# A GEGLU and spectral-mixing kernel: one product of the next chunk moved into the tail of the down projection, part of the down projection moved ahead of the last gate/up product, and silu of the last chunk by one ACT function

## The chip, the cores and the metric

The kernel runs on one core of a Trainium2 chip. The metric is the device time of one execution in microseconds (us). The kernel before the change took 1782.99 us (median of 3 runs, 1782.35 to 1784.18). The engines are called as in the profile: PE multiplies matrices (PEld is its weight load), DVE is the vector engine, ACT the activation engine, POOL the second, slower vector engine, and SP the queue that issues nearly all DMAs.

## The reference

The input x has 8192 tokens of 448 values. With xn the layer norm of x, the result is

```
s = irfft(shrink(mlp(rfft(xn over the tokens))))        # block-diagonal complex MLP, 4 blocks of 112
g = silu((gelu(xn @ w_gate) * (xn @ w_up)) @ w_down)    # 448 -> 1792 -> 448
out = x + s * g
```

Everything is float32. The kernel reaches float32 accuracy with float16 matmuls: each operand is split into a high and a low half, and a product takes three matmuls (high by high, high by low, low by high).

## The kernel before, in words

**Work.** The 8192 tokens are laid out as 128 x 64, and a *chunk* is 4 of the 64 columns, 512 tokens; there are 16 chunks, numbered i = 0 to 15. The FFN runs in two parts over the hidden units: part p = 0 has hidden blocks 0 to 7 (of 128), part p = 1 blocks 8 to 13. Part 0 of all chunks comes first and leaves partial sums in DRAM (`prt`); part 1 reads them back (tile `pt`), adds its own, and gives silu. From some point of part 0 on, both the gate/up projections and the down projection use a fast scheme with 7 instead of 8 block products.

**Gate/up** (`unit`, line 1108). Two hidden blocks make a unit; part 1 has 3 units in a chunk. A unit's 7 products are the generators a1, a5, a6, a4, a2, a3, a7. They accumulate in two PSUM banks, X (ring `bx`) and Y, Z (ring `by`), and between them ACT or DVE work on the banks: `seed` copies X after a1, `sum5` adds after a6 (DVE, `by<-bx,u`), `c22` adds after a7 (DVE, `v<-bx,u`), and a4 adds into X only when that addition has read it. After a4 comes gelu, the multiplication by up, and `sums` (line 1208), which makes the left operands of the down projection. A product on the X side that reads tile `xta` is 12 matmuls of 256 columns; one that reads `xtb` (a2, a3, a4) is 10.

**Down** (`down2`, line 1355, and `prod2`, line 1322). The 7 products are prod2(1) to prod2(7); each has 6 matmuls of 224 columns for each unit of the chunk. They accumulate in banks x and y (ring `bd`) and z (ring `by`). Banks are read in the middle: `add2` (DVE, `pt<-bd`) adds the bank to the partial sum of one quadrant of the chunk, and after that the next product adds on into the same bank. The part called `tail` is not run at the end of the chunk but within the next one, after a1 and a5 of its first unit: it finishes prod2(6) in bank x and prod2(5) in bank y, then waits for `add2` of x, and goes on with prod2(7) in x, prod2(3) in y and prod2(4) in x. Each quadrant that is complete goes to `ended2` (line 1454): `add2`, then tanh by ACT on half the value, and (1 + tanh) times the half by DVE, which is silu. The last chunk has no next one, so its tail follows at once, and its last product is cut in two halves (`last_half`, line 1437).

**Side work.** The spectral branch runs beside the FFN in three phases that fill gaps: phase 1 (layer norm, first DFT stage, operands of the FFN, one chunk each `DT` us from `T1` on), phase 2 (second DFT stage, MLP, shrinkage, third stage; 64 tasks spread evenly up to `END2`), and phase 3 (last DFT stage, multiplication by silu, adding x, the store; spread up to `END3`). In phase 3, chunks whose FFN is done by then take silu from DRAM (`gsp`) in tiles of two columns; later chunks multiply at once (`gate`, line 1422), called direct here.

**What sets the order.** Nothing is scheduled by the compiler. The kernel writes every engine's instructions in the order of a plan: `Pace` (line 50) runs the generators as tasks against a model of the engines (line 172) and of DMA (line 136), and the order in which they reach an instruction is the order on the engine. Each engine then runs its list in order and waits on semaphores. The choice of DVE or POOL for an operation written as `B.` (line 209) is the plan's too. So any change of a constant of the plan may reorder the side work everywhere after it.

Of the kernel before, what the change touches and what calls it, by code (L numbers as in the profile page):

```python
# [13 lines left out]
AF = mybir.ActivationFunctionType  # L14
ALU = mybir.AluOpType
# [6 lines left out]
NG = 16  # L22
# [7 lines left out]
PF = ((0, 8), (8, 6))  # L30
# [19 lines left out]
class Pace:  # L50
# [85 lines left out]
    def issue(self, e, op, out, ins, run):  # L136
        outs, ins, start = self.start(e, out, ins)
        if e == "SP" or op == "dma_start":
            size = (outs or ins)[0].nbytes()
            self.dma = max(self.dma, start) + size / 320e3  # L140
            if op == "dma_start_transpose":
                self.free[e] = start + 1.15 + size / 380e3
                end = max(self.free[e] + 2.6, self.dma + 1.5)
            else:
                self.free[e] = start + 0.5
                end = max(start + 2.2 + size / 240e3, self.dma + 1.5) + (2.5 if outs and start > 100.0 else 0.0)
        else:
            end = start + self.cost(e, op, start, out, ins)
            self.free[e] = end
            if self.shares(e, op, out, ins):  # L150
                self.port[e] = self.port[e][-11:] + [(start, end)]
        for i in ins:
            self.note(i, False, end, e)
        for o in outs:
            self.note(o, True, end, e)
        self.last = max(self.last, end)
        return run()
# [234 lines left out]
def afno_geglu_kernel(ctx, tc, x, gu, wd, mlp, b1, b2, c_m, c_mt, c_small, out):  # L392
# [4 lines left out]
    B = Either(pace, V, G, 0.0)  # L397
# [32 lines left out]
    def pe():  # L430
        return pace.free.get("PE", 0.0) - 0.3
# [16 lines left out]
    wt = [cp.tile([128, 2, 16, 128], F16, name=f"wt{f}") for f in range(PF[0][1])]  # L448
    dw = [cp.tile([128, PF[0][1], D], F16, name=f"dw{i}") for i in range(2)]
    ms = cp.tile([128, 32], F32, name="ms")  # L450
    cB = [fb[:, 0:1], fb[:, 1:2]]
    cF = ms[:, 24:25]

# [209 lines left out]
            if c + 1 < NG + PL:  # L663
                yield ev("phase", c)

    T1, DT = 84.0, 37.0


    def gu_loads(fs, again):
# [411 lines left out]
    state = {"direct": NG}  # L1081
# [26 lines left out]
    def unit(p, i, f0, h, xa, seven):  # L1108
# [87 lines left out]
        def c21():  # L1196
            gl = yield from (GL if p == 0 else GL2).get()
            gelu(p, f0, gl, m["X"])
            BX.put(m["X"])
            yield  # L1200
            yield from glu(p, seven, f0, gl, m["v2"], 1, h, lambda: V2.put(m["v2"]))
            if seven:
                yield from sums(gl)
                return
            GL.put(gl)
            done("h", p, i, f0, 1)
# [148 lines left out]
    def down2(p, i, h, last):  # L1355

        n = PF[p][1] // 2
        yield from last()
        x = yield from BD.get()
        yield from prod2(1, p, i, h, x, 0, n - 1, first=True)  # L1360
        z = yield from BY.get()
        yield from prod2(2, p, i, h, z, 0, n - 1, first=True)
        T.matmul(z[:, 2 * DH:], h[:, 0, 0, 0:128], dw[0][:, 0, 0:512 - 2 * DH], start=False, stop=False,
                 skip_group_check=True)
        y = yield from BD.get()
        yield from prod2(5, p, i, h, y, 0, n - 2, first=True)
        yield from prod2(1, p, i, h, x, n - 1, n)
        e = pace.spawn(add2(p, i, QS[0], x), pace.last)
        yield from prod2(2, p, i, h, z, n - 1, n, last=True)
        pace.spawn(ended2(p, i, QS[0], z, BY, e), pace.last)  # L1370
        yield from prod2(5, p, i, h, y, n - 2, n - 1)
        yield e
        yield from prod2(6, p, i, h, x, 0, n - 1)

        def tail():
            yield from prod2(6, p, i, h, x, n - 1, n)
            e = pace.spawn(add2(p, i, QS[2], x), pace.last)
            yield from prod2(5, p, i, h, y, n - 1, n)
            e5 = pace.spawn(add2(p, i, QS[1], y), pace.last)
            yield e  # L1380
            yield from prod2(7, p, i, h, x, 0, n)
            pace.spawn(ended2(p, i, QS[1], x, None), pace.last)
            yield e5
            yield from prod2(3, p, i, h, y, 0, n, last=True)
            pace.spawn(ended2(p, i, QS[2], y, BD), pace.last)
            yield ev("u3", p, i)
            if p == 0 or i < NG - 1:
                yield from prod2(4, p, i, h, x, 0, n, last=True)
                pace.spawn(ended2(p, i, QS[3], x, BD), pace.last)
                return  # L1390
            tf = yield from TH.get()
            for t in range(2):
                yield from prod2(4, p, i, h, x, 0, n, last=True, halves=(t,))
                pace.spawn(last_half(i, QS[3], x, tf, t), pace.last)

        state["tail"] = tail
# [40 lines left out]
    def last_half(i, qq, b, tf, a):  # L1437

        v = slice(a, a + 1)
        q, s4 = EV["ptb", i, qq][:, v], blk(state["last"], *qq)[:, v]  # L1440
        x4 = EV["lgt", i, qq[0]][-1][:, v, DH * qq[1]:DH * qq[1] + DH]
        th = tf.rearrange("p (a d) -> p a d", a=2)[:, v]
        V.scalar_tensor_tensor(q, part(b, 128, 2, DH)[:, v], cB[1], q, op0=ALU.mult, op1=ALU.add)
        yield
        S.activation(th, q, AF.Tanh)
        B.tensor_mul(s4, q, s4)
        yield
        V.scalar_tensor_tensor(th, th, 1.0, s4, op0=ALU.add, op1=ALU.mult)
        yield
        B.tensor_add(th, th, x4)  # L1450
        yield
        Q.dma_start(blk(ov[:, CH * i:CH * i + CH, :], *qq)[:, v], th)

    def ended2(p, i, qq, b, R, earlier=None):

        if earlier:
            yield earlier
        if p == 1 and state["direct"] <= i < NG - 1:
            pace.spawn(gate_bank(i, qq))
        yield from add2(p, i, qq, b)  # L1460
        if R:
            R.put(b)
        else:
            done("u3", p, i)
        if p == 0:
            t, v = EV["ptb", 0, i, qq]
            Q.dma_start(blk(chunk_of(prt, i), *qq), v)
            TH.put(t)
            return
        q = EV["ptb", i, qq]  # L1470
        tf = yield from TH.get()
        th = tf.rearrange("p (a d) -> p a d", a=2)
        S.activation(th, q, AF.Tanh)
        if i < NG - 1:
            yield
            V.scalar_tensor_tensor(th, th, 1.0, q, op0=ALU.add, op1=ALU.mult)
            PT.put(q)
            yield
            if i >= state["direct"]:
                yield from gate(i, qq, th)  # L1480
                Q.dma_start(blk(ov[:, CH * i:CH * i + CH, :], *qq), th)
                TH.put(tf)
                return
            Q.dma_start(blk(chunk_of(gsp, i), *qq), th)
            TH.put(tf)
            EV["gn", i] = EV.get(("gn", i), 0) + 1
            if EV["gn", i] == 4:
                done("gsp", i)
            return
        for a in range(qq[0], CH, 2):  # L1490
            yield ev("s4", a)
        yield ev("lg", i, qq[0])
        yield ev("hs", 1, i, PF[1][1] - 2, 0)
        s4, x4 = blk(state["last"], *qq), EV["lgt", i, qq[0]][-1][:, :, DH * qq[1]:DH * qq[1] + DH]
        B.tensor_mul(s4, q, s4)
        yield
        V.scalar_tensor_tensor(th, th, 1.0, s4, op0=ALU.add, op1=ALU.mult)
        yield
        V.tensor_add(th, th, x4)
        PT.put(q)  # L1500
        yield
        Q.dma_start(blk(ov[:, CH * i:CH * i + CH, :], *qq), th)
        TH.put(tf)
# [78 lines left out]
    def chunk(p, i):  # L1582
# [26 lines left out]
        for u, (_, a5, a6, a4, a2, a3, a7) in enumerate(units):  # L1609
            yield from a5()  # L1610
            yield pe()
            if u == 0 and "tail" in state:
                yield from state.pop("tail")()
                if (p, i) == (1, 0):
                    factors_in(1)
                    open_mq()
                    pace.spawn(xt_load(nxt[1], "a", nxt[0]))
                    pace.spawn(pt_loads(i))
            yield from a6()
            yield pe()  # L1620
            if u == 0:
                yield ev("xt", "b", p, i)
            else:
                yield from prev()
                if (p, i) == (0, NG - 1):
                    pace.spawn(far_pair(u - 1))
                yield pe()
            yield from a2()
            yield pe()
            for s in (a3, units[u + 1][0], a7) if u + 1 < len(units) else (a7, a3) if seven else (a3, a7):  # L1630
                yield from s()
                yield pe()
            prev = a4
# [300 lines left out]

            pace.spawn(store())

    END1, END2, END3 = T1 + NG * DT + 12.0, 1460.0, 1765.0

    def phase2():
        yield ev("phase1")  # L1940
# [445 lines left out]
```

## Time and profile before

| | before |
|---|---|
| median of 3 runs | 1782.99 us |
| the profiled execution's own time | 1784.63 us |
| its span, first to last instruction | 1782.8 us |
| granted clock of PE | 0.997 |
| PE, share of the span busy | 99% |
| DVE | 78% |
| ACT | 58% |
| POOL | 32% |
| DMA, mean rate | 160 GB/s |

The span leaves out what lies around the first and last instruction; the execution's own time is 1.8 us longer. All lines of helper calls have one line number (204), so the groups are told apart by the names of their tiles. A row of a timeline gives start, duration, engine, operation, tiles, number merged, and in brackets the idle time of the engine before it and what ended that. PE's matmul ends are modelled; the idle time of PEld shows more directly how long PE's stream stood still.

### The profile page before, as it was taken

Reading aid. Unit: us, or ns where it says so; the run is one execution under the profiler, and the core shown is the slowest. Engines: PE = TensorE matmul, PEld = TensorE weight load, DVE = VectorE, ACT = ScalarE, POOL = GpSimd, SP = SyncE. Lnnn points to the kernel's source line nnn. Section 1 sums busy time; section 2 is a strip of 40 time slices with the busy share of each in tenths; the row PEclk is TensorE's granted clock in tenths of the full one; section 3 lists DMA queues with packets and bytes.
Section 4 is the critical chain, followed back from the end, with each engine's and each line's share of the span. In section 5 each row is a group of like instructions: output and inputs, shape, how many; then the busy total and the mean of one; then the engine's idle time right before and its main releaser. Section 6 shows DMA issues by size and latency. Waiting matters only on the chain.

```text
span 1782.8 us, 40305 instructions
## 1 busy us (share of the span) xinstructions
PE 1759.6 (99%) x16183; PEld 1470.3 (82%) x16183; DVE 1392.9 (78%) x2471; ACT 1031.5 (58%) x2019; POOL 570.4 (32%) x689
## 2 busy tenths in 40 slices
PE   8999999999999999999999999999999999999998
PEld 4447677777787799999999999999999998988887
DVE  7879777777776676767778788888888887888877
ACT  6646555546555545666767666777666663333333
POOL 3153444555542542222212123333132321121211
PEclk9999999999999999999999999999999999999999
DMA  6465776677766653323147554434354438999871
GB/s 216 133 179 166 185 217 181 189 225 202 214 188 178 182 141 82 79 64 90 53 100 208 156 121 111 109 90 103 92 121 110 99 96 262 285 294 306 260 263 53
DMA packets 354892, 285.37 MB, mean 160 GB/s; under 512 B 235184, under 2 KB 324784, under 8 KB 354704
## 3 DMA queue, kind: packets, MB, share of 16 engines
q1 hardware_dynamic: 354416, 282.24, 55.8%
q8 instruction: 126, 2.06, 0.5%
q14 instruction: 62, 0.51, 0.1%
q10 hardware_dynamic: 288, 0.56, 0.1%
HBM read 128.36 MB, written 105.23 MB: 131 GB/s over the span
## 4 chain that ended last, share of the span: by engine, by line
PE 93%; DVE 4%; DMA 1%; ACT 1%; issue 1%; POOL 0%; SPq 0%; ACTq 0%; DVEq 0%; POOLq 0%
PE bx L204 31%; PE by L204 23%; PE bd L204 22%; PE bf L204 16%; DVE wt L204 1%; DMA prt<-th 1%; DVE g L204 1%; DVE pt L204 1%; ACT wt L204 0%; SPq L204 0%; DMA out<-th 0%; DVE v L204 0%; DVE th L204 0%; DMA x<-in_x 0%; ACT th L204 0%
## 5 line engine op out<-in xcount | busy, mean ns | idle before, releaser
L204 PEld LDWEIGHTS <-wt 128*128 128x128 f16 x9350 | 906.7, 98 | 172.3 <-issue 16.7
L204 PE MATMUL bx<-xta,wt 128*128 128x256 f16 (+1 forms) x3843 | 476.2, 275 | 3.0 <-ACT by L204 1.2
L204 PEld LDWEIGHTS <-h 128*128 128x128 f16 x2710 | 260.1, 98 | 83.5 <-issue 2.4
L204 PE MATMUL bd<-dw,h 128*128 128x448 f16 (+1 forms) x1596 | 254.1, 310 | 1.1 <-DVE pt L204 0.8
L204 PE MATMUL by<-xtb,wt 128*128 128x256 f16 x2080 | 252.6, 273 | 2.0 <-DVE by L204 2.0
L204 PE MATMUL by<-xta,wt 128*128 128x256 f16 (+1 forms) x1347 | 177.2, 279 | 0.8 <-DVE xta L204 0.8
L204 POOL TENSOR_TENSOR wt<-wt 128x256 f32<-128x256 f32 x80 | 63.1, 789 | 297.8 <-DVE wt L204 279.8
L204 PE MATMUL bx<-xtb,wt 128*128 128x256 f16 x1040 | 130.5, 272 | 1.8 <-DVE v L204 1.8
L204 DVE TENSOR_TENSOR by<-bx,u 128x512 f32<-128x512 f32 x104 | 72.5, 697 | 61.9 <-PE bx L204 53.0
L204 ACT COPY u<-by 128x512 f32<-128x512 f32 x104 | 60.8, 584 | 86.3 <-PE by L204 86.0
L204 POOL TENSOR_TENSOR zs<-t,zs 112x256 f16<-112x256 f32 (+1 forms) x38 | 31.7, 835 | 243.5 <-ACT zs L204 243.5
L204 PE MATMUL bd<-dw,wt 128*128 128x224 f16 (+1 forms) x816 | 99.4, 264 | 2.7 <-DVE pt L204 2.5
L204 ACT ACTIVATE u<-by,fc 128x512 f32<-128x512 f32 (+1 forms) x118 | 73.6, 635 | 49.2 <-PE by L204 49.0
L204 ACT CAST h<-wt 128x512 f16<-128x512 f32 (+1 forms) x128 | 68.6, 536 | 48.8 <-DVE wt L204 40.1
L204 DVE TENSOR_TENSOR v<-bx,u 128x512 f32<-128x512 f32 x104 | 71.4, 686 | 21.5 <-PE bx L204 20.4
L204 ACT COPY by<-bx 128x512 f32<-128x512 f32 x104 | 59.7, 574 | 44.9 <-PE bx L204 44.4
L204 PE MATMUL bf<-w2t,wn 112*128 112x112 f16 x1512 | 84.9, 213 | 0.0
L204 DVE SCALAR_TENSOR_TENSOR pt<-bd,fb,pt 128x448 f32<-128x448 f32 (+1 forms) x97 | 65.0, 675 | 23.7 <-PE bd L204 22.9
L204 PEld LDWEIGHTS <-wn 112*128 112x128 f16 x1512 | 80.6, 98 | 1.0
L204 ACT ACTIVATE th<-pt 128x448 f32<-128x448 f32 (+1 forms) x65 | 37.1, 571 | 73.9 <-DVE pt L204 67.7
L204 ACT ACTIVATE th<-bd,fb 128x448 f32<-128x448 f32 x62 | 39.1, 633 | 64.8 <-PE bd L204 62.8
L204 ACT ACTIVATE gl<-bx,fc 128x512 f32<-128x512 f32 (+1 forms) x70 | 40.6, 600 | 56.8 <-PE bx L204 49.8
(263 smaller groups left out, 3332.2 us busy)
## 6 DMA issues: line engine op xcount, KB each, us to landing
xts<-sx SPq DMA_DIRECT2D x32, 480.0 KB, 3.9
x<-in_x SPq DMA_DIRECT2D x17, 896.0 KB, 6.3
t<-ysb SPq DMA_DIRECT2D x64, 224.0 KB, 3.1
prt<-th SPq DMA_DIRECT2D x64, 224.0 KB, 2.5
pt<-prt SPq DMA_DIRECT2D x64, 224.0 KB, 3.8
u<-t SPq DMA_DIRECT2D x32, 448.0 KB, 5.9
x<-in_x SPq DMA_DIRECT2D x32, 448.0 KB, 6.4
y<-t SPq DMA_DIRECT2D x30, 448.0 KB, 3.6
```

Of the source, the lines that this page charges most:

```text
L204: return self.pace.issue(self.name, kind, out, ins, lambda: fn(out, *args, **kw))
```

## The change

1. In `down2`, the first unit's share of prod2(1), 6 matmuls into bank x, is put ahead of `last()`, which is a4 of the chunk's last unit. It came after it.
2. In `tail`, the next chunk's a6 (of its first unit) is put between prod2(5) and the wait for `add2` of x. It came after the whole tail. The last chunk's tail has no such product.
3. In the last chunk silu is one ACT function on the half value with scale 2, then a multiplication by the spectral factor and an addition of x, both by DVE. Before, it was tanh, a multiplication of the half value by the spectral factor (DVE or POOL), (1 + tanh) times that, and the addition (DVE or POOL). An ACT instruction on one column, put after the last gelu, brings in the function's table.
4. Constants of the plan: loads are modelled as landing 0.5 us later, `DT` goes from 37.0 to 36.5, `END2` from 1460 to 1480. `END3` stays at 1765.

```diff
-                end = max(start + 2.2 + size / 240e3, self.dma + 1.5) + (2.5 if outs and start > 100.0 else 0.0)
+                end = max(start + 2.2 + size / 240e3, self.dma + 1.5) + (3.0 if outs and start > 100.0 else 0.0)
...
-    T1, DT = 84.0, 37.0
+    T1, DT = 84.0, 36.5
...
+            if (p, i, f0) == (1, NG - 1, PF[1][1] - 2):
+                S.activation(fb[:, 4:5], mhalf1, AF.Silu)
...
+        x = yield from BD.get()
+        yield from prod2(1, p, i, h, x, 0, 1, first=True)
         yield from last()
-        x = yield from BD.get()
-        yield from prod2(1, p, i, h, x, 0, n - 1, first=True)
+        yield from prod2(1, p, i, h, x, 1, n - 1)
...
-        def tail():
+        between = []
+
+        def tail(mid=None):
+            between.extend([mid] if mid else [])
             yield from prod2(6, p, i, h, x, n - 1, n)
             e = pace.spawn(add2(p, i, QS[2], x), pace.last)
             yield from prod2(5, p, i, h, y, n - 1, n)
             e5 = pace.spawn(add2(p, i, QS[1], y), pace.last)
+            if between:
+                yield from between[0]()
+                yield pe()
             yield e
...
-        S.activation(th, q, AF.Tanh)
-        B.tensor_mul(s4, q, s4)
-        yield
-        V.scalar_tensor_tensor(th, th, 1.0, s4, op0=ALU.add, op1=ALU.mult)
-        yield
-        B.tensor_add(th, th, x4)
+        S.activation(th, q, AF.Silu, scale=2.0)
+        yield
+        V.tensor_tensor(th, th, s4, op=ALU.mult)
+        yield
+        V.tensor_tensor(th, th, x4, op=ALU.add)
...
-        S.activation(th, q, AF.Tanh)
+        S.activation(th, q, AF.Silu if i == NG - 1 else AF.Tanh, scale=2.0 if i == NG - 1 else 1.0)
...
-        B.tensor_mul(s4, q, s4)
-        yield
-        V.scalar_tensor_tensor(th, th, 1.0, s4, op0=ALU.add, op1=ALU.mult)
-        yield
-        V.tensor_add(th, th, x4)
+        yield
+        V.tensor_tensor(th, th, s4, op=ALU.mult)
+        yield
+        V.tensor_tensor(th, th, x4, op=ALU.add)
...
-            if u == 0 and "tail" in state:
-                yield from state.pop("tail")()
+            ahead = u == 0 and "tail" in state
+            if ahead:
+                yield from state.pop("tail")(a6)
...
-            yield from a6()
-            yield pe()
+            if not ahead:
+                yield from a6()
+                yield pe()
...
-    END1, END2, END3 = T1 + NG * DT + 12.0, 1460.0, 1765.0
+    END1, END2, END3 = T1 + NG * DT + 12.0, 1480.0, 1765.0
```

More of the change, by code (lines that the diff above doesn't have):

```diff
@@ L450, in afno_geglu_kernel @@
     ms = cp.tile([128, 32], F32, name="ms")
+    mhalf1 = mhalf[:, 0:1]
     cB = [fb[:, 0:1], fb[:, 1:2]]
```

## The prediction, on record before the result

> **What bounds the kernel now.** I read the page first: who is busy.
>
> ```profile
> PE 1759.6 (99%) x16183; PEld 1470.3 (82%) x16183; DVE 1392.9 (78%) x2471; ACT 1031.5 (58%) x2019; POOL 570.4 (32%) x689
> ```
>
> PE is the bound: 1759.6 of 1782.8 us. The change adds and removes no matmul, so it can win only what PE stands still, and what follows PE's last matmul. Next, the busy time of long stretches: two of phase 2, then phase 3, then the end (us, then busy time and count of PE, PEld, DVE, ACT, POOL, clock, DMA share, GB/s).
>
> ```profile
> 712.00:1112.00 400.00, 399.59 (x4348) 369.34 (x4346) 310.01 (x563) 270.10 (x562) 97.50 (x99) 1.00 0.42 109
> 1112.00:1472.00 360.00, 358.78 (x3899) 331.62 (x3898) 302.42 (x529) 245.62 (x500) 105.94 (x106) 1.00 0.43 104
> 1472.00:1732.00 260.00, 256.19 (x2353) 227.97 (x2351) 210.46 (x334) 94.65 (x166) 52.24 (x59) 1.00 0.90 278
> 1732.00:1783.00 51.00, 43.20 (x404) 38.74 (x402) 36.77 (x63) 19.09 (x34) 6.52 (x8) 0.97 0.26 82
> ```
>
> The clock is full. In phase 3 DMA is busy at 0.90 where it was at 0.43, and DVE at 210.46/260 = 0.81. PE's idle time is small, so the third view is what PEld waited for, from 630 to 1472 us and then from 1472 to 1735 us (us in total, times, longest).
>
> ```profile
> PEld L204 <- issue: 3.9, 11, 0.8
> ...
> PEld L204 <- issue: 5.3, 9, 1.8
> ```
>
> So PE stood still for 9.2 us in 20 places over the stretch in which the scheme of 7 products runs. I followed each in the timeline. They are of three kinds: 8 stand in the tail of the down projection, 3 before the a4 of a chunk's last unit, and 9 elsewhere. The change goes at the first two kinds.
>
> **The tail (part 2).** The pace of matmuls comes from two pieces of the chain that ended last: 24 of 256 columns in 2.62 us, 0.109 us each; 18 of 224 columns in 1.73 us, 0.096 us each.
>
> ```profile
> 1733.22 1.73 PE bd L204 x18
> ...
> 1741.87 2.62 PE bx L204 x24
> ```
>
> A typical tail, PE and then DVE:
>
> ```profile
> 1592.35 1.31 PE L204 MATMUL bd<-wt,h 128*128 128x224 f16 x12
> 1593.87 0.35 PE L204 MATMUL bd<-dw,wt 128*128 128x224 f16 x2 [0.20 <-DVE pt L204]
> ```
>
> ```profile
> 1593.13 1.28 DVE L204 SCALAR_TENSOR_TENSOR pt<-bd,fb,pt 128x448 f32<-128x448 f32 x2 [0.43 <-PE bd L204]
> ```
>
> The 12 matmuls are prod2(6) in x and prod2(5) in y. After the first 6 (0.57 us) DVE may read x; it starts at 1593.13 and its first addition takes half of 1.28 us. But prod2(5) covers only 0.57 us of it, and 12 x 0.096 = 1.15 us after 1592.35 PE is out of work, at 1593.50. It goes on at 1593.87: 0.37 us lost. The 8 such places, the first and the last (PEld's rows, idle time in brackets):
>
> ```profile
> 652.57 0.48 PEld L204 LDWEIGHTS <-h 128*128 128x128 f16 x5 [0.31 <-issue]
> ...
> 1730.19 0.86 PEld L204 LDWEIGHTS <-wt 128*128 128x128 f16 x9 [0.36 <-issue]
> ```
>
> Two are of 0.31 (part 0), six of 0.36 to 0.38: 2.8 us. Between them lie tails without a wait, in which the plan happened to put a matmul of the side work there. The change puts a6 there: 12 x 0.109 = 1.31 us, over three times what is missing, so all 8 go, even with DVE almost 1 us late. What is late next? a6 itself needs only `seed`, done long before; its `sum5` puts one more DVE addition (about 0.7 us) into the tail, behind both `add2`, and a3 needs it five products later. Bank y's `add2` gains the same cover. a2 now follows prod2(4) at once and needs Z and `xtb`, whose load was issued a whole down projection earlier. prod2(7), 3, 4 and their stores come 1.31 us later. I cost these at nothing: nothing in the next 4 us of PE waits for them. **-2.8 us.**
>
> **The head (part 1).** PE, DVE and PEld before an a4, the last with the first such place too:
>
> ```profile
> 1624.91 1.25 PE L204 MATMUL by<-xtb,wt 128*128 128x256 f16 x10
> 1626.59 0.60 PE L204 MATMUL bx<-xtb,wt 128*128 128x256 f16 x4 [0.43 <-DVE v L204]
> ```
>
> ```profile
> 1625.86 0.68 DVE L204 TENSOR_TENSOR v<-bx,u 128x512 f32<-128x512 f32 x1
> ```
>
> ```profile
> 639.32 0.75 PEld L204 LDWEIGHTS <-wt 128*128 128x128 f16 x7 [0.36 <-issue]
> ...
> 1626.60 0.97 PEld L204 LDWEIGHTS <-wt 128*128 128x128 f16 x9 [0.60 <-issue]
> ```
>
> a4 has to wait until DVE has read X (`v<-bx,u`, end 1626.54), and a3 alone is 1.09 us of cover. Six matmuls of prod2(1) add 0.57 us. The three waits (0.36, 0.36 and 0.60) make 1.32 us, of which 0.03 stays: **-1.3 us**. The operands of prod2(1) come from the first unit and bank x has been free since the tail, so nothing is newly waited for; a4's own results come 0.57 us minus the saved wait later, and the next tail, which needs them, has a1 and a5 (2.6 us) ahead of it.
>
> **The last chunk (parts 1 to 3).** Here no next chunk covers the tail. PEld waited 0.36 us for the same a4:
>
> ```profile
> 1761.54 0.53 PEld L204 LDWEIGHTS <-wt 128*128 128x128 f16 x5 [0.36 <-issue]
> ```
>
> With 0.57 us in front a4 starts 0.21 us later, and the chain of waits at the end runs through what follows a4 (gelu, `sums`, tail): **+0.2 us**. On ACT the rows after that a4, and the only table load of the trace:
>
> ```profile
> 1763.07 0.69 ACT L204 ACTIVATE wt<-bx,fc 128x512 f32<-128x512 f32 x1
> 1764.86 0.41 ACT L204 CAST h<-wt 128x256 f16<-128x256 f32 x1 [1.10 <-DVE wt L204]
> 1765.77 0.62 ACT L204 CAST h<-wt 128x512 f16<-128x512 f32 x1 [0.51 <-DVE wt L204]
> ```
>
> ```profile
> 1.65 1.28 ACT L204 ACT_TABLE_LOAD   x1 [1.65 <-PEq L2377]
> 2.95 0.20 ACT L204 ACTIVATE fb<-mhalf 128x1 f32<-128x1 f32 x1
> ```
>
> The new instruction follows the gelu. Load and one column take 1.28 + 0.20 = 1.48 us and the gap is 1.10, so the first cast is 0.38 us late; the second has 0.51 us to spare, so 0.13 us is left over: nothing. The Trainium skill (ScalarE: Activation LUTs, section "What ACT_TABLE_LOAD costs") gives a drain of about 1.38 us on top of the 1283 ns. The trace shows the 1283 ns, and behind it the next instruction at once; no run here shows a load in the middle of work. By the page the second cast would be 1.25 us late, and the sum 1.25 us higher.
>
> The end, on DVE and POOL (the last matmul starts at about 1776.6):
>
> ```profile
> 1776.64 0.38 DVE L204 TENSOR_TENSOR s<-pt,s 128x224 f32<-128x224 f32 x1
> 1776.94 0.44 DVE L204 SCALAR_TENSOR_TENSOR pt<-bd,fb,pt 128x224 f32<-128x224 f32 x1
> 1777.30 1.38 DVE L204 SCALAR_TENSOR_TENSOR th<-th,s 128x448 f32<-128x448 f32 x2
> 1778.61 0.91 DVE L204 TENSOR_TENSOR th<-th,x 128x448 f32<-128x448 f32 x2
> 1779.44 0.38 DVE L204 SCALAR_TENSOR_TENSOR th<-th,s 128x224 f32<-128x224 f32 x1
> 1779.86 0.39 DVE L204 TENSOR_TENSOR th<-th,x 128x224 f32<-128x224 f32 x1
> ```
>
> ```profile
> 1777.46 0.98 POOL L204 TENSOR_TENSOR s<-pt,s 128x224 f32<-128x224 f32 x1 [1.22 <-DVE pt L204]
> ```
>
> From `pt` on DVE needs 3.31 us (1776.94 to 1780.25), and POOL's 0.98 us lies within it. After the change the last half needs pt 0.44, silu (as tanh of this size, about 0.4; silu isn't in the trace, and I take it between that and twice that), a multiplication 0.38 and an addition 0.39: 1.6 us and some 0.1 for hand-offs, so up to 1.6 us less. If DVE still has to do the two additions before (0.91 in the rows) it is 2.6 us, 0.7 us less. I take **-1.0 us**, with -1.6 and, by a doubled silu in all three dependent places, +0.2 as ends.
>
> **The plan (part 4).** Phase 2 ends 20 us later and starts about 8 us earlier (16 x 0.5), so its 64 tasks thin out by about 4%; the five of the 9 others that lie before 1472 us sum to about 1.8 us (3.9 less 1.7 in tails and 0.36 before an a4), and I take **-0.3**. Phase 3 has the same work in 240 instead of 260 us: DMA 0.90 x 260/240 = 0.97, DVE 0.81 to about 0.84. The four remaining waits there sum to 3.2 us (5.3 less 1.1 and 0.96), the largest of them this one, where ACT waited for a store, DVE for ACT, and PE for DVE:
>
> ```profile
> 1693.88 0.58 ACT L204 ACTIVATE th<-pt 128x448 f32<-128x448 f32 x1 [3.50 <-DMA out<-th]
> ```
>
> ```profile
> 1695.77 0.31 PEld L204 LDWEIGHTS <-wt 128*128 128x128 f16 x3 [1.80 <-issue]
> ```
>
> I let them grow by a quarter, **+0.8**; bounds are -1.6 (half of them vanish in a new order) and +9 (below). The 0.5 us on loads only puts their users later in the order: 0, since no wait of PE on DMA stands in the trace. Phase 1's order before 215 us is drawn anew as well; I take 0, within 2 us either way.
>
> **The sum.** -2.8 - 1.3 + 0.2 - 1.0 - 0.3 + 0.8 = -4.4 us. From the profiled execution, 1784.63 to 1780.2. The median lies 1.64 us below that execution: 1782.99 - 4.4 = 1778.6 us.
>
> **Rivals.**
> *DVE is the real bound of the tails.* If DVE, at 0.81 in phase 3, gets to `add2` over 1 us late, the wait stays in front of prod2(7), or moves to a3. For it: rows show DVE starting an addition late elsewhere. Against: at 1593.13 DVE was idle for 0.43 us before it. It takes back the 2.8 us and leaves 1781.4.
> *Phase 3 is too tight: slower.* Stores land later at a DMA share of 0.97, all three buffers of `th` are in flight, ACT stops as at 1693.88, and each such stop costs PE 1.80 us. From one stop in each of the five direct chunks (10 to 14) on it decides: 5 x 1.80 = 9.0 against -5.2 for the rest, 1786.8. For it: DMA at 0.90 already. Against: one stop in 20 stores before, and moving the quadrants 1.31 us apart from the first gives its store more time.
> *The table load is longer, or is on the path.* Every microsecond beyond the gap is paid at the end. With a second load's worth, 1.28 us, it is 1779.9. The page's drain comes to about the same.
> *The stage boundary flips.* Ten chunks take silu from DRAM:
>
> ```profile
> gsp<-th SPq DMA_DIRECT2D x40, 224.0 KB, 2.5
> ```
>
> 40 stores, four a chunk. If phase 3 begins after chunk 10's start, an eleventh follows: 1.8 MB more, at 278 GB/s 6.6 us of DMA, PE's work unchanged. I count it to the slower rival's causes.
>
> **How the numbers follow.** Forecast (both covers hold, 1774 to 1781) 0.62; DVE bound 0.16, at 1781.4; phase 3 too tight 0.13, at 1786.8; table load 0.09, at 1779.9. A measurement here can tell about 0.2%, 3.6 us. Faster by more (below 1779.4): 0.60 of the forecast, 0.03 of the table load and 0.03 of the DVE case, 0.66; slower by more (above 1786.6) half or more of the third, 0.10; the same 0.24. The range leaves out about 2 in 10: from 1773.5 (the end at -1.6, waits halved and 2 us in phase 1) to 1783.0 (DVE bound and 1.6 us of phase 3).
>
> **What would show it.** Right: no PEld wait between prod2(5) and prod2(7) but in the last tail; `bx<-xta` as 12 matmuls there; no wait before the last unit's a4; one more table load; under 3 us from the last `pt` to the last addition; 40 stores to `gsp`. Wrong: waits on `pt` or `by` after 1490 us that sum to over 8 us, ACT waiting for `out<-th` several times, or new waits between 84 and 630 us.

## The result, and the profile after

| | before | after |
|---|---|---|
| median | 1782.88 us (6 runs, 1782.03 to 1784.18) | 1776.34 us (6 runs, 1775.42 to 1776.92) |
| ratio | | 0.9963, 95% interval 0.9950 to 0.9976 |
| the profiled execution's own time | 1784.63 us | 1775.42 us |
| its span | 1782.8 us | 1773.6 us |

The change makes the kernel 6.5 us faster by the medians; 4.4 were forecast, and 1776.34 lies within the range. Mind the two profiled executions: that of before lies 1.75 us above its median, that of after 0.92 below, so the traces differ by 9.2 us and about 2.7 of that is the spread of executions.

The page after, its first line:

```profile
PE 1758.0 (99%) x16183; PEld 1469.4 (83%) x16183; DVE 1401.5 (79%) x2482; ACT 1032.0 (58%) x2021; POOL 532.5 (30%) x673
```

PE has as many matmuls and all but the same busy time. DVE has 11 instructions more and POOL 16 fewer. The gain is PE's idle time and the end. The stretches after, with phase 3 now from 1494 us on:

```profile
712.00:1112.00 400.00, 399.86 (x4333) 369.45 (x4331) 312.79 (x558) 270.79 (x558) 86.63 (x100) 1.00 0.43 108
1112.00:1494.00 382.00, 381.71 (x4135) 352.90 (x4134) 323.75 (x561) 258.42 (x524) 99.63 (x107) 1.00 0.42 103
1494.00:1732.00 238.00, 237.50 (x2199) 212.54 (x2197) 196.01 (x318) 85.02 (x150) 42.83 (x49) 1.00 0.96 293
1732.00:1774.00 42.00, 35.59 (x326) 31.20 (x324) 32.04 (x54) 17.85 (x32) 6.90 (x9) 0.97 0.37 126
```

In phase 3 the share of DMA went from 0.90 to 0.96 (0.97 was worked out), and yet PE's idle time there fell from 3.8 us (260.00 less 256.19) to 0.5. What PEld waited for, 630 to 1494 us and 1494 to 1728 us:

```profile
PEld L204 <- issue: 1.3, 6, 0.3
...
PEld L204 <- issue: 0.8, 2, 0.6
```

2.1 us in 8 places, where there were 9.2 in 20. Here is a tail, the one that the prediction showed at 1592 us before, PE and then DVE:

```profile
1585.23 1.31 PE L204 MATMUL bd<-wt,h 128*128 128x224 f16 x12
1586.38 1.47 PE L204 MATMUL bx<-xta,wt 128*128 128x256 f16 x12
1587.69 0.73 PE L204 MATMUL bf<-u,mt 128*128 128x448 f16 x3
1588.26 1.31 PE L204 MATMUL bd<-dw,wt 128*128 128x224 f16 x12
```

```profile
1586.01 1.28 DVE L204 SCALAR_TENSOR_TENSOR pt<-bd,fb,pt 128x448 f32<-128x448 f32 x2 [0.91 <-PE bd L204]
1587.97 0.70 DVE L204 TENSOR_TENSOR by<-bx,u 128x512 f32<-128x512 f32 x1 [0.68 <-PE bx L204]
```

DVE starts the same two additions 0.78 us after the 12 matmuls begin, as before, and needs the same 1.28 us. But PE has a6 (`bx<-xta`) to do, and prod2(7) (`bd<-dw,wt`) finds its bank read: the first addition ended at 1586.69. The added `by<-bx,u` comes behind both, as forecast.

This tail also holds 3 matmuls of the side work (`bf<-u,mt`), and so do 14 of the 15 tails that part 1 of the FFN has ahead of the last chunk's. Before, tails with side work didn't wait either, so the zero of this kernel alone proves little; the experiments decide it. Its one tail with nothing but a6, PE and then DVE, goes through as well:

```profile
1500.05 1.31 PE L204 MATMUL bd<-wt,h 128*128 128x224 f16 x12
1501.20 1.47 PE L204 MATMUL bx<-xta,wt 128*128 128x256 f16 x12
1502.51 1.31 PE L204 MATMUL bd<-dw,wt 128*128 128x224 f16 x12
```

```profile
1500.83 1.28 DVE L204 SCALAR_TENSOR_TENSOR pt<-bd,fb,pt 128x448 f32<-128x448 f32 x2 [1.59 <-PE bd L204]
```

**Where the time went.** For every two neighbouring matmuls I took the interval of their starts, less the median interval of that shape, and sorted the excess by what PE was about to do. With the piece from the last matmul's start to the end, the sum is what the profiled execution takes above 1746.7 to 1747.2 us, in all fourteen executions that I took apart this way. So the table accounts for the differences to 0.5 us (us; in brackets the number of waits over 0.14 us):

| | before | after | parts 1, 2 | part 2 | part 1 | part 3 | part 4 | 1st null | 2nd null |
|---|---|---|---|---|---|---|---|---|---|
| tail, before prod2(7) | 3.00 (9) | 0 | 0.36 (1) | 0 | 5.76 (14) | 2.99 (9) | 1.61 (5) | 4.52 (13) | 3.83 (12) |
| a4 of a last unit | 2.46 (5) | 0.21 (1) | 0.30 (1) | 3.59 (7) | 0 | 2.46 (5) | 1.13 (4) | 2.03 (5) | 1.13 (4) |
| a4 within a chunk | 0.35 (1) | 0.62 (1) | 0.31 (1) | 1.84 (3) | 0.30 (1) | 0.35 (1) | 0.92 (2) | 0.61 (1) | 0.85 (2) |
| a2 or a3 | 1.95 (2) | 0 | 0 | 0 | 1.42 (2) | 2.01 (2) | 1.01 (1) | 0.28 (1) | 1.60 (2) |
| prod2(6) after the first `add2` | 1.60 (3) | 0.83 (3) | 2.16 (4) | 1.54 (3) | 0.51 (1) | 1.58 (3) | 0.51 (1) | 1.71 (3) | 1.27 (3) |
| side work | 0.16 (1) | 0.58 (3) | 1.42 (2) | 0.40 (1) | 0.48 (2) | 0.16 (1) | 1.34 (3) | 0.96 (3) | 1.55 (4) |
| last chunk, after its a4 | 1.76 (3) | 2.00 (3) | 1.83 (3) | 1.76 (3) | 2.54 (4) | 1.89 (3) | 1.76 (3) | 1.76 (3) | 1.76 (3) |
| waits under 0.14 us | 1.43 | 1.28 | 1.57 | 1.29 | 1.46 | 1.44 | 1.44 | 1.34 | 1.29 |
| last matmul to the end | 6.43 | 4.78 | 6.56 | 6.87 | 6.45 | 4.78 | 6.44 | 6.44 | 6.44 |
| 45 to 630 us | 6.34 (5) | 6.73 (9) | 5.85 (5) | 6.24 (5) | 5.39 (5) | 5.86 (5) | 7.04 (10) | 6.28 (7) | 8.07 (8) |
| the first 45 us | 12.4 | 11.2 | 11.8 | 12.2 | 11.6 | 11.1 | 11.8 | 12.4 | 11.7 |

The columns on the right are experiments, told next. The first row holds every wait in a tail up to the start of prod2(7). Nearly all stand right before prod2(7); some stand within prod2(6) and wait for its operand `h`, which a6 comes too late to cover: the one of parts 1 and 2 (0.36 us), two of part 1 (0.97 together) and one in each null (0.49 and 0.16). The first 45 us differ by over 1 us with the same order of instructions (before and part 3), so they tell of the execution and not of the kernel. The waits after 630 us come back in the next execution: before and part 3 share their order up to the last chunk, and their first seven rows agree within 0.15 us.

### The profile page after: what moved, and what is told of

The parts are those of the page before. It is cut to its first block, busy times and chain, and to the rows that moved or that the text cites. A ratio compares the mean times of both kernels' runs of the same rounds, so it can differ in the third digit from the quotient of the medians.

```text
span 1773.6 us, 40295 instructions
## 1 busy us (share of the span) xinstructions
PE 1758.0 (99%) x16183; PEld 1469.4 (83%) x16183; DVE 1401.5 (79%) x2482; ACT 1032.0 (58%) x2021; POOL 532.5 (30%) x673
## 4 chain that ended last, share of the span: by engine, by line
PE 93%; DVE 4%; ACT 1%; DMA 1%; issue 1%; POOL 0%; SPq 0%; ACTq 0%; DVEq 0%; POOLq 0%
PE bx L204 31%; PE by L204 24%; PE bd L204 22%; PE bf L204 16%; DVE wt L204 1%; DVE h L204 1%; DVE g L204 0%; DVE pt L204 0%; DMA wst<-in_down 0%; DMA ident<-c_small 0%; DVE v L204 0%; DVE c L204 0%; ACT h L204 0%; ACT wt L204 0%; DMA xts<-xs 0%
## 5 line engine op out<-in xcount | busy, mean ns | idle before, releaser
L204 PE MATMUL bd<-dw,h 128*128 128x448 f16 (+1 forms) x1596 | 257.9, 310 | 2.2 <-DVE pt L204 0.9
L204 POOL TENSOR_TENSOR zs<-t,zs 112x256 f16<-112x256 f32 (+1 forms) x35 | 25.1, 716 | 205.0 <-ACT zs L204 204.8
L204 POOL TENSOR_TENSOR sx<-sf,sx 128x128 f16<-128x128 f32 (+2 forms) x72 | 60.6, 863 | 46.8 <-ACT sx L204 44.0
```

The costliest lines, as they stand in the source:

```text
L204: return self.pace.issue(self.name, kind, out, ins, lambda: fn(out, *args, **kw))
```

## The experiments

The difference given with each run is worked out from its ratio and the time of before beside it, which was measured together with it. The ratio isn't that of the two medians, which can differ from it by up to 1 us.

My theory was that the two covers take away their waits, the silu shortens the end, and the constants do little. The rivals: the constants do it; any change draws a new order of the side work, and the gain is luck; the waits only move; the table load is on the path.

### The parts by themselves

**e1: parts 1 and 2**, the changed hunks of `down2`, `tail` and `chunk`, all else as before.

```diff
+        yield from prod2(1, p, i, h, x, 0, 1, first=True)
         yield from last()
+        yield from prod2(1, p, i, h, x, 1, n - 1)
...
+            if between:
+                yield from between[0]()
+                yield pe()
...
```

> Parts 1 and 2 alone (six matmuls of prod2(1) ahead of a4, a6 within the tail); tanh and all constants as before. Theory 'covers': the waits in the 8 tails (2.8 us) and before the 3 a4 (1.3 us) go and the rest stays as it was, so 3 to 4.5 us less than before, and PEld shows no wait between prod2(5) and prod2(7) but in the last tail. Rival 'constants': the moves give at most 1.5 us, since the waits only move. Rival 'redrawn order': anything within 3 us of before, with the sum of the other waits changed by as much as the covers bring.

Measured: 1779.03 us against 1783.70, ratio 0.9974 (0.9965 to 0.9983), 4.6 us less. One wait in a tail is left, and it is for `h` from POOL; before prod2(7) none is left but in the last chunk. The large wait of 1.80 us, which began with a store, is gone too, with the constants of before. "Constants" falls: it allowed the moves 1.5 us at most.

**e2: part 3**, silu in the last chunk, all else as before.

```diff
-        S.activation(th, q, AF.Tanh)
-        B.tensor_mul(s4, q, s4)
+        S.activation(th, q, AF.Silu, scale=2.0)
+        V.tensor_tensor(th, th, s4, op=ALU.mult)
```

> Part 3 alone: silu by one ACT function in the last chunk; order up to there as before. Theory 'covers': 0.7 to 1.6 us less, all of it after PE's last matmul, with the table load at 1.3 us and no drain behind it. Rival 'table load on the path': 0 to 1.3 us more, PE waiting longer for the operands of prod2(6).

Measured: 1781.60 against 1783.70, ratio 0.9991 (0.9982 to 1.0000), 1.6 us less, at the edge of the noise. It is the cleanest of the runs, since the order before the last chunk stays. The end piece falls from 6.43 to 4.78 us, by 1.65. On ACT:

```profile
1761.64 0.69 ACT L204 ACTIVATE wt<-bx,fc 128x512 f32<-128x512 f32 x1
1762.35 1.28 ACT L204 ACT_TABLE_LOAD   x1
1763.64 0.20 ACT L204 ACTIVATE fb<-mhalf 128x1 f32<-128x1 f32 x1
1763.75 0.39 ACT L204 CAST h<-wt 128x256 f16<-128x256 f32 x1
1764.35 0.62 ACT L204 CAST h<-wt 128x512 f16<-128x512 f32 x1 [0.21 <-DVE wt L204]
```

The load starts as gelu ends and takes 1.28 us; the next instruction starts 0.01 us later. The cast after it is late, but the second cast still waits 0.21 us for DVE: the load found room.

**e3: part 4**, the three constants, all else as before.

```diff
+                end = max(start + 2.2 + size / 240e3, self.dma + 1.5) + (3.0 if outs and start > 100.0 else 0.0)
+    T1, DT = 84.0, 36.5
+    END1, END2, END3 = T1 + NG * DT + 12.0, 1480.0, 1765.0
```

> Part 4 alone: loads modelled 0.5 us later, DT 36.5, END2 1480. Theory 'covers': within 1.5 us of before, the waits in tails and before a4 still there. Rival 'constants': 3 us or more less, with phase 3's other waits (3.2 us before) nearly gone. Rival 'redrawn order': within 3 us either way.

Measured: 1782.28 against 1783.70, ratio 0.9992 (0.9984 to 1.0001): 1.4 us less, and no difference is within the interval. Five tail waits and four before a last unit's a4 remain. Phase 3's crowding is seen on ACT, which waits for a store three times and not once, but PE pays only 1.01 us for it:

```profile
ACT th L204 <- DMA out<-th: 6.0, 3, 2.5
```

**e4: the changed kernel with the constants of before**, so parts 1 to 3.

```diff
-    T1, DT = 84.0, 36.5
+    T1, DT = 84.0, 37.0
...
```

(and the other two lines of e3 taken back).

> The changed kernel with the three constants of before (parts 1, 2 and 3). Theory 'covers': 4 to 6 us less than before, so within 1.5 us of the changed kernel. Rival 'constants': 1 to 2.5 us less than before, 4 or more above the changed kernel.

Measured: 1777.41 against 1783.70, ratio 0.9970 (0.9962 to 0.9979), 5.4 us less. The changed kernel has 0.9963 (0.9950 to 0.9976). What the constants add beside the rest, about 1 us, isn't clear of noise.

**e5: part 2 alone**, a6 within the tail.

```diff
+            if between:
+                yield from between[0]()
+                yield pe()
```

> Part 2 alone: a6 of the next chunk within the tail. Theory 'covers': the 8 waits in tails go, 2.8 us less than before, and the 3 before a4 (1.3 us) stay; the large wait near 1694 us, after a store, may go too, since the quadrants move apart, which makes 4.6. Rival 'redrawn order': within 3 us of before either way, with as much won or lost outside the tails.

Measured: 1781.86 against 1783.43, ratio 0.9994 (0.9985 to 1.0002), 1.1 us less: a miss. No tail wait is left, and none of a2 or a3. But the waits before a4 have grown. PE's waits from 630 to 1735 us, of this kernel and then of before:

```profile
PE bx L204 <- DVE v L204: 3.7, 9, 0.7
PE bd L204 <- DVE pt L204: 1.0, 3, 0.4
```

```profile
PE bd L204 <- DVE pt L204: 2.3, 9, 0.4
PE bx L204 <- DVE v L204: 1.6, 5, 0.7
PE by L204 <- DVE by L204: 1.6, 1, 1.6
```

**e6: part 1 alone**, six matmuls of prod2(1) ahead of a4.

```diff
+        yield from prod2(1, p, i, h, x, 0, 1, first=True)
         yield from last()
+        yield from prod2(1, p, i, h, x, 1, n - 1)
```

> Part 1 alone: six matmuls of prod2(1) ahead of a4 of the last unit. Theory 'covers': the 3 waits before a4 go, 1.3 us less than before (0.2 more in the last chunk), the 8 in tails stay. Rival 'redrawn order': within 3 us either way.

Measured: 1784.11 against 1783.43, ratio 1.0006 (0.9997 to 1.0015), 1.1 us more: a miss as well. The waits before a last unit's a4 are all gone, but the tails have 14 waits instead of 9, 5.76 us instead of 3.00. So neither part alone is worth what its row gave, and together they are worth more than the sum of both. That called for the next runs.

### How much a new order is worth by itself

**e8: a first null**, a change of one constant that means nothing.

```diff
-    T1, DT = 84.0, 37.0
+    T1, DT = 84.0, 37.05
```

> The kernel before with DT at 37.05, a change that means nothing but lets the plan choose anew. Theory 'covers': within 1.5 us of before, the sum of the waits in tails and before a4 at 3 to 5 us as before, if in other chunks. Rival 'redrawn order': up to 3 us either way, so that the gain of the change can't be told from chance.

Measured: 1784.44 against 1783.43, ratio 1.0006 (0.9997 to 1.0015). Thirteen tail waits, 4.52 us.

**e10: a second null.**

```diff
-                end = max(start + 2.2 + size / 240e3, self.dma + 1.5) + (2.5 if outs and start > 100.0 else 0.0)
+                end = max(start + 2.2 + size / 240e3, self.dma + 1.5) + (2.55 if outs and start > 100.0 else 0.0)
```

> The kernel before with loads modelled 0.05 us later, a second change that means nothing. If the order before was an ordinary draw: within 1.5 us of before, 8 to 10 tail waits. If it was a lucky one, as the first such run suggests (13 tail waits of 4.5 us where before has 9 of 3.0): 0.5 to 2.5 us slower than before, with 11 or more tail waits.

Measured: 1787.15 against 1783.41, ratio 1.0022 (1.0013 to 1.0031), 3.9 us slower, more than either expectation had, from nothing but another order: 12 tail waits, a large wait of a3 again (1.16 us, the row below; ACT had waited 2.83 us for a store), and new waits before 630 us (8.07 against 6.34 us in the table).

```profile
1652.90 1.25 PE L204 MATMUL by<-xtb,wt 128*128 128x256 f16 x10 [1.16 <-DVE by L204]
```

Of four new orders without the tail's cover (part 1, part 4, the nulls) tail waits number 5 to 14, 1.6 to 5.8 us; before, with 9 and 3.0 us, lay in the better half. Which tails wait depends on whether the plan puts matmuls of the side work into them. In these five orders I sorted the 15 tails that each has in part 1 of the FFN ahead of the last chunk, 75 in all: 33 have no side work between prod2(6) and prod2(7), and all 33 wait; 42 have some, and one waits. With a6 there the plan leaves 19 tails without side work in seven kernels (after, e1, e4, e5, e7, e9 and e11; e4 repeats e1's order), and none of them waits. So a6 does what the side work did by chance. That accounts for part 1 alone: it took its own waits away and drew an order with more tail waits.

**e11: parts 1 and 2 with a new order.**

```diff
-    T1, DT = 84.0, 37.0
+    T1, DT = 84.0, 37.05
```

(on e1's kernel).

> Parts 1 and 2 with DT at 37.05 and all else as before: a fresh order for the covered kernel. Theory 'both covers together': 3.5 to 6 us less than before, at most one wait each in tails and before a last unit's a4. Rival 'lucky order': the gain of parts 1 and 2 shrinks to under 2.5 us.

Measured: 1778.90 against 1783.41, ratio 0.9975 (0.9964 to 0.9985), 4.5 us less, as e1. No tail wait and none before a last unit's a4. Under the constant of e8 the covered kernel keeps its gain: 1778.90 us where e8 took 1784.44.

**e7: the changed kernel with DT back at 37.0.**

```diff
-    T1, DT = 84.0, 36.5
+    T1, DT = 84.0, 37.0
```

> The changed kernel with DT at 37.0 again (END2 and the loads as changed). The changed kernel has 2.4 us of waits between 215 and 630 us that the kernel before doesn't have. If the denser phase 1 makes them, they go: 1 to 2.5 us less than the changed kernel, and this is the fastest. If the later landing of loads in the plan makes them, or they come with any new order, the time is within 1 us of the changed kernel.

Measured: 1777.78 against 1783.43, ratio 0.9970 (0.9960 to 0.9980). The waits before 630 us don't go but change places (one of 1.73 us at 255 us), 7.7 us in all against 6.7. The denser phase 1 doesn't make them, and this isn't a faster version.

**e9: half the cover in the tail.** The first block of a6 stays in the tail, the second comes behind it.

```diff
-                yield from state.pop("tail")(a6)
+                yield from state.pop("tail")(lambda: a6((0,)))
...
-            if not ahead:
-                yield from a6()
-                yield pe()
+            yield from a6((1,) if ahead else (0, 1))
+            yield pe()
```

> The changed kernel with only half of a6 (6 matmuls, 0.65 us) within the tail and the other half behind it. Theory 'both covers together': a tail lacks about 0.36 us, so half the cover is enough; no tail waits but in the last chunk, and the time within 1.5 us of the changed kernel. Rival 'the full length matters, since it sets the quadrants and their stores apart': waits for stores return in phase 3, 1 to 3 us more than the changed kernel.

Measured: 1778.99 against 1783.41, ratio 0.9973 (0.9963 to 0.9983). No tail waits in any chunk but the last, and 7 of the 15 of part 1 hold nothing but the half of a6: 0.65 us is cover enough. The intervals of this ratio and of the changed kernel's overlap; a2 and a3 wait 0.89 us where they wait for nothing in the changed kernel. Whether the full length is worth another 1 or 2 us stays open.

**e12: silu without the instruction that brings the table in.**

```diff
-            if (p, i, f0) == (1, NG - 1, PF[1][1] - 2):
-                S.activation(fb[:, 4:5], mhalf1, AF.Silu)
```

(on e2's kernel).

> Part 3 alone without the instruction that brings the table in, so that the load stands before the first silu of the last chunk. Theory 'the load has room': ACT is idle there for over 1 us, and this first quadrant isn't the last to be stored, so within 0.5 us of part 3 alone. Rival 'the load is on the path': 1 to 1.5 us more than part 3 alone, or 2.7 with a drain.

Measured: 1782.43 against 1783.41, ratio 0.9994 (0.9986 to 1.0003), against 0.9991 for e2: the times can't tell the two apart, but the traces can. The load stands before the first silu of 448 columns, between two instructions that were ready:

```profile
1766.33 0.62 ACT L204 CAST h<-wt 128x512 f16<-128x512 f32 x1 [0.71 <-POOL wt L204]
1766.97 1.28 ACT L204 ACT_TABLE_LOAD   x1
1768.26 0.58 ACT L204 ACTIVATE th<-pt 128x448 f32<-128x448 f32 x1
```

DVE has a multiplication for that silu ahead of the tail's `add2`, so it stops, and PE stops before prod2(7). DVE and PE in e12, then PE in e2:

```profile
1768.87 0.63 DVE L204 TENSOR_TENSOR th<-th,s 128x448 f32<-128x448 f32 x1 [0.67 <-ACT th L204]
1769.41 0.68 DVE L204 SCALAR_TENSOR_TENSOR pt<-bd,fb,pt 128x448 f32<-128x448 f32 x1
```

```profile
1770.14 1.31 PE L204 MATMUL bd<-dw,wt 128*128 128x224 f16 x12 [0.75 <-DVE pt L204]
```

```profile
1768.94 1.31 PE L204 MATMUL bd<-dw,wt 128*128 128x224 f16 x12 [0.20 <-DVE pt L204]
```

That wait is 0.92 us by the account of intervals where it is 0.36 in e2, and the end piece is the same (4.79 and 4.78 us). So about 0.55 us of the 1.28 us load reaches PE here, which neither the theory (room) nor the rival (1 to 1.5 us) had; the early instruction saves that.

## Why the prediction was right, and where it was not

**PE's standing still is all there is to win: right.** The accounts close to 0.5 us without any change in the pace of matmuls.

**The tail, -2.8: right** in kind and size between the two traces (3.00 to 0), and the cause is shown by the count of tails without side work (33 of 33 wait without a6, 0 of 19 with it). What the step left out is that 2.8 was the value of one order. In the other orders without the cover those waits, less the ones for `h`, came to 1.6 to 4.8 us; the same cover should be worth that there, but only e8's constant was run both ways.

**The head, -1.3: the term was too small.** The part did what the prediction said, but a fourth wait, 0.78 us at 1347 us with side work between a3 and a4, was counted among the "9 elsewhere"; it stands before a last unit's a4 as well. Without the last chunk these waits went from 2.11 to 0.21 us, -1.9.

**The last chunk, +0.2: about right.** The wait before its a4 (0.35) is gone and the waits behind grew from 1.76 to 2.00, which is -0.1. The tail there still waits for `add2` and, for 1.1 us, for the read of half a bank, as it has no next chunk to take work from.

**The end, -1.0: mis-sized, -1.65 measured** (in e4 and e9 about -1.35)**,** where -1.6 was the bound that I gave for DVE free of other work. The rows of after:

```profile
1768.81 0.62 DVE L204 TENSOR_TENSOR th<-th,x 128x448 f32<-128x448 f32 x1
1769.35 0.45 DVE L204 SCALAR_TENSOR_TENSOR pt<-bd,fb,pt 128x224 f32<-128x224 f32 x1
1769.71 0.38 DVE L204 TENSOR_TENSOR th<-th,x 128x224 f32<-128x224 f32 x1
1770.25 0.39 DVE L204 TENSOR_TENSOR th<-th,s 128x224 f32<-128x224 f32 x1 [0.16 <-ACT th L204]
1770.67 0.39 DVE L204 TENSOR_TENSOR th<-th,x 128x224 f32<-128x224 f32 x1
```

From `pt` to the last addition it is 1.71 us (1769.35 to 1771.06) where it was 3.31: the quadrant before is done, and the addition of the first half fits into silu's time. Silu costs what tanh does, 0.58 us for 448 columns.

**The table load, 0: right,** by e2, where the last tail's wait for `h` stayed at 0.44 us. It depends on the place: the later load of e12 cost PE about 0.55 us. The Trainium skill (ScalarE: Activation LUTs, section "What ACT_TABLE_LOAD costs") adds a drain of about 1.38 us to each switch to a different set. The traces don't agree: in e2, e12 and after the load follows the instruction before it within 0.02 us, and the next starts 0.01 us behind it, so a switch costs 1.28 us.

**The plan, +0.8 in phase 3 and -0.3 before: wrong in sign, and this is where the forecast and the traces part most.** I let the four other waits in phase 3 grow from 3.2 us by a quarter, because DMA would be at 0.97. DMA went to 0.96, and those waits fell to 0.6. (By the same ratio DVE's 0.81 would have been put at 0.88 and not at 0.84; it was 0.82, 196.01 of 238.00.) Of the 1.8 us before 1472 us, 0.78 stood before a last unit's a4 and 0.16 in a tail; the rest grew from 0.86 to 1.30 us. The 1.80 us are the largest share, and the traces show where they went. DVE's queue of before at that place:

```profile
1694.48 0.62 DVE L204 SCALAR_TENSOR_TENSOR th<-th,pt 128x448 f32<-128x448 f32 x1 [1.85 <-ACT th L204]
1695.03 0.69 DVE L204 TENSOR_TENSOR by<-bx,u 128x512 f32<-128x512 f32 x1
```

The first waits for ACT's tanh, which waits for a store; the second is `sum5` of the new chunk's first unit. It needs nothing of that tanh but stands behind it, and a3 stands behind `sum5`. A stop of the same kind after the change, ACT, then PE, then DVE:

```profile
1640.75 0.58 ACT L204 ACTIVATE th<-pt 128x448 f32<-128x448 f32 x1 [2.48 <-DMA out<-th]
```

```profile
1639.07 2.35 PE L204 MATMUL by<-xtb,wt 128*128 128x256 f16 x20
```

```profile
1633.02 0.70 DVE L204 TENSOR_TENSOR by<-bx,u 128x512 f32<-128x512 f32 x1
```

ACT stops for a store as before, but `sum5` was done 7 us earlier, since a6 comes early in the tail, and a2 and a3 (20 matmuls) run through. With all of a6 in the tail ACT stops five times in phase 3 for a store of `out`, in after (2.5 us), e1 (1.5), e4 (2.6) and e7 (1.7 and 2.5), and no a3 waits 1 us or more. With the old tail there are eight such stops, in before (3.5 us), e3 (three, 6.0), e6 (two, 4.5) and e10 (two, 5.7). One in each kernel made an a3 wait 1.0 to 1.8 us, all four with the DVE rows shown above; at the others the plan had put `sum5` ahead of the waiting multiplication, or the stop was short (1.1 us). e5, e8 and e11 have no such stop. e9 also stops (2.5 and 3.8 us) without such a wait, but half of its a6 and so its `sum5` still come behind the tail; there it is the plan's order. So an early `sum5` is the cause that the rows show, but counts of five and eight don't rule out that a new order alone would have done the same. I had looked at what `sum5` adds to the tail, and not at what it no longer stands behind. The thought that the quadrants would be further apart, which I set against a rival, isn't needed, and the stops don't bear it out. Phase 1's 0 within 2 us held (+0.4).

**The rivals.** "DVE is the real bound of the tails" fell for the pair and for the tail. For part 2 alone it may hold elsewhere: e5 waits longer before a4 (5.4 us with those within chunks) than any kernel with the old order of the head (2.0 to 2.8). Whether PE, once it no longer stops in tails, runs into DVE at the next place, or whether that was one more draw, stays open. "Phase 3 is too tight" fell: e3 shows more stops of ACT for stores, as that rival had it, but PE pays 1.0 us for them, and nothing in the kernels with all of a6 in the tail. The boundary stayed: 40 stores to `gsp`. That the gain is the luck of an order fell too: the six kernels with both covers, in five orders (e4 repeats e1's up to the last chunk), took 1776.3 to 1779.0 us, and the eight without one or both 1781.6 to 1787.2.

In sum, between the traces: tails -3.0, a4 of last units -2.2 with the last chunk's, the end -1.65, a2 and a3 -1.95, all other waits together +0.4, the first 45 us -1.15: 9.6 us, beside 9.2 between the two executions. By the medians it is 6.5, so the forecast of 4.4 fell short by 2.1 us. Of the other 2.7 us, 1.15 lie in the first 45 us; where the rest lies, one trace of each kernel can't tell.

## What to carry to other kernels

On an engine that is busy all the time, look for the few places where its stream must wait for another engine's read of what it has just written, and put independent work of known length there: 0.65 us of it took away waits of 0.36 us in all 7 tails that held nothing else (e9), and 1.31 us in 12 more over six kernels. Before a gain of 0.1 to 0.2% is believed in a kernel whose order a plan works out, run one or two changes that mean nothing: here one moved it by 0.22% and the other by 0.06% (not clear of zero), as much as each part alone. What is moved forward also leaves the queues that it stood in: look at what it no longer waits behind. And judge covers together: a part alone may be hidden by the order that it draws.

## What was not expected of the hardware

A table load in the middle of ACT's work took ACT 1.28 us and no more, and silu from the new table as much as tanh (0.58 us for 448 columns). The order of the instructions fixes the waits: two executions on different kernels with the same order had the same waits at the same places, most of them to 0.02 us; the a3 wait behind a store varied more (1.79, 1.86 and 2.09 us in before, e2 and e12), and only the first 45 us by over 1 us.
